# Attention and gated MLP in split fp32: a seventh pair of blocks by seven products, and edge rows kept in DRAM until the last batch

## The chip, the cores and the metric

One Trainium2 chip, one core. The metric is device time in microseconds of one execution. A lower time is better. Several runs were taken of the kernel before, and one more execution of it was profiled.

## The reference

Attention over 32 packed rows, then a gated MLP over all 4608 tokens, in fp32:

```python
p_packed = sm_attn(p, k, v)            # batch 8, heads 8, seq 576, dim 64, 32 packed rows
out = sm_attn(q, p_packed, p_packed)
x = out.transpose(0, 2, 1, 3).reshape(4608, 512)
h = x @ w_in                           # 512 x 2048
g = h * clip(h + 3, 0, 6) / 6
result = g @ w_out                     # 2048 x 512
```

## The kernel before

Each fp32 operand of a product is split into a high part and a rest (`split`: ScalarE casts the high part, L946, GpSimd subtracts it, L947), and one product becomes three matmuls: high by high, high by rest, rest by high. For each batch b the input side of the MLP is folded into the attention: `u_m` multiplies quarters of `w_in` (L350 matmuls on a tile named `w_again`) with the packed rows, so that `first_product` (L929) yields h from the attention weights of the batch. The hidden dimension of 2048 is 16 blocks f of 128.

A batch has 576 tokens. They are taken in two chunks c of 256 tokens; the 64 left over ride along in one chunk, which is then "wide" (320 columns in the first product): c = 0 in odd batches, c = 1 in even ones. The 64 last rows of an even batch and the 64 first of the next odd one make one tile of 128 "edge" rows, whose second product is done apart. After the gate (`gate_into`: ScalarE's relu L940, VectorE's product L941) `keep_edge` (GpSimd, L965) copies the 64 columns into `bnd`, 16 blocks by 128 columns of SBUF. For a pair of batches the tile `bnd` fills over a wide chunk of each of the two.

A chunk (`moe_pairs`, batch 1's second chunk to batch 7) runs over 16 steps, one block f each: first product, gate, split, and, one or two steps later (`pend`, `second`), the second product. Two consecutive blocks form a pair, whose second product goes by seven products instead of eight (`pair_product`, 21 matmuls of 256 columns, L969, into four PSUM banks A to D). That needs sums of the gated tiles (VectorE L1241, L1249, L1254) and sums of blocks of `w_out` (T1 to T4, made once by `combine`). `PAIRS` = 6 pairs run first, 0 to 5, or 5 to 0 where `down(b, c)` holds, which lets the last pair of one chunk be the first of the next; then the four blocks 12 to 15 come as singles (`single_product`, 6 matmuls of 512 columns each). Batch 1's second chunk has four pairs. First products alternate between two PSUM buffers, so the first product of a step can start only when the gate of two steps before has read its bank.

The combinations are made during batch 1, in steps that the table `TURN` gives (its numbers are steps of batch 1, 16 to a chunk; each entry advances the generator by one yield). A combination has 11 VectorE instructions, 4 casts on ScalarE (L1076) and 2 sums on GpSimd (L1072). T blocks of pairs 0, 1, 4 and 5 share two places in SBUF and are swapped through DRAM (`t_kept`, fetched by `fetch_t`, L1105, at the chunk positions in `FETCHES`).

SP issues all DMAs from one queue in the order written. Eight DMA semaphores go round: a DMA also waits for the one eight before it. The quarters of `w_in` for the next batch are fetched one at a time into one place (`w_again`, L1428), each when TensorE is done with the one before.

The edge products: batches 0 and 1 in batch 1's first chunk; batches 2 and 3 in the singles of batch 3's wide chunk ("joined", a bank J of its own, two blocks at a time through `edge_parts` and `edge_product`); batches 4 and 5 are written to DRAM (`e_kept`, one transfer of 1 MB in batch 5) and read back in batch 7, where `moe_edges`, after the first chunk of batch 7, multiplies them together with those of 6 and 7, as two tiles by the same scheme of pairs and singles.

Attention for the next batch is woven in by `fill`, called at each step, which also advances `turned` (the combinations), the fetches and `u_m` of the batch.

## Time and profile before

| | us |
|---|---|
| median of 3 runs | 711.25 |
| lowest, highest | 711.24, 712.88 |
| the profiled execution | 710.69 |
| its span | 708.8 |

| engine | busy us | share |
|---|---|---|
| TensorE, matmul (PE) | 684.8 | 97% |
| TensorE, weight load (PEld, beside PE) | 591.5 | 83% |
| VectorE (DVE) | 522.9 | 74% |
| ScalarE (ACT) | 428.3 | 60% |
| GpSimd (POOL) | 406.8 | 57% |

Times in the profile are microseconds from the span's start unless marked ns. A row of the timeline gives start, length, engine, line and operation; in brackets the idle time ahead of it and who ended it. A row of the chain gives start, length, engine and line of a piece of the chain that ended last. A group row ends in busy time and mean ns of one, then the idle time ahead. Batch 2 begins at about 210, its second chunk at 256, the second chunk of batch 4 at 423.

### The profile page before, as it was taken

Reading aid. Unit: us, or ns where it says so; the run is one execution under the profiler, and the core shown is the slowest. Engines: PE = TensorE matmul, PEld = TensorE weight load, DVE = VectorE, ACT = ScalarE, POOL = GpSimd, SP = SyncE. Lnnn points to the kernel's source line nnn. Section 1 sums busy time; section 2 is a strip of 40 time slices with the busy share of each in tenths; the row PEclk is TensorE's granted clock in tenths of the full one; section 3 lists DMA queues with packets and bytes.
Section 4 is the critical chain, followed back from the end, with each engine's and each line's share of the span. In section 5 each row is a group of like instructions: output and inputs, shape, how many; then the busy total and the mean of one; then the engine's idle time right before and its main releaser. Section 6 shows DMA issues by size and latency. Waiting matters only on the chain.

```text
span 708.8 us, 16225 instructions
## 1 busy us (share of the span) xinstructions
PE 684.8 (97%) x5924; PEld 591.5 (83%) x5924; DVE 522.9 (74%) x1125; ACT 428.3 (60%) x1004; POOL 406.8 (57%) x617
## 2 busy tenths in 40 slices
PE   6599999999999999999999999999999999999997
PEld 4377877777877888899798998898888988899996
DVE  2897788688998759775588867877597768766653
ACT  5788876455655655565366655656475655565553
POOL 2565542545644566576375746776464656676763
PEclk9799999999999999999999999999999999999999
DMA  9999853955247656464554648375655644340330
GB/s 276 288 242 244 225 124 126 260 142 130 100 143 173 161 136 209 123 170 74 133 183 144 165 88 252 120 149 137 194 203 147 167 125 150 134 164 1 120 119 30
DMA packets 199678, 111.15 MB, mean 157 GB/s; under 512 B 173488, under 2 KB 185264, under 8 KB 195760
## 3 DMA queue, kind: packets, MB, share of 16 engines
q1 hardware_dynamic: 199056, 109.94, 55.8%
q8 instruction: 46, 0.75, 0.4%
q14 instruction: 32, 0.26, 0.1%
q10 hardware_dynamic: 544, 0.20, 0.1%
HBM read 92.27 MB, written 17.83 MB: 155 GB/s over the span
## 4 chain that ended last, share of the span: by engine, by line
PE 84%; DVE 7%; DMA 5%; ACT 1%; POOL 1%; issue 1%; SPq 1%; DVEq 0%; ACTq 0%
PE acc L969 49%; PE ps_hh L929 23%; PE ps L350 6%; PE ps_h L607 3%; DMA w_again<-w_kept 2%; DMA room<-in_q_dram 1%; PE ps L470 1%; DMA wt<-t_kept 1%; PE ps L440 1%; DVE wt L1077 1%; DVE tr L555 1%; DMA p_nat<-in_p_dram 1%; DMA nat<-in_k_dram 1%; PE ps L273 1%; SPq L294 0%
## 5 line engine op out<-in xcount | busy, mean ns | idle before, releaser
L929 PE MATMUL ps_hh<-a_lo,m_hi 128*128 128x320 f32 (+1 forms) x448 | 133.6, 298 | 0.0
L929 PE MATMUL ps_hh<-a_hi,m_hi 128*128 128x320 f32 (+1 forms) x448 | 133.5, 298 | 0.0
L929 PE MATMUL ps_hh<-a_hi,m_lo 128*128 128x320 f32 (+1 forms) x448 | 132.6, 296 | 0.0
L941 DVE SCALAR_TENSOR_TENSOR t<-t,ps_hh 128x320 f32<-128x320 f32 (+1 forms) x148 | 65.8, 445 | 57.8 <-ACT t L940 57.1
L969 PE MATMUL acc<-wo_hi,g 128*128 128x512 f32 x304 | 108.3, 400 | 0.0
L940 ACT ACTIVATE t<-ps_hh,three 128x320 f32<-128x320 f32 (+1 forms) x148 | 73.4, 499 | 43.8 <-PE ps_hh L929 32.4
L947 POOL TENSOR_TENSOR ge<-t,ge 128x256 fp32r<-128x256 f32 x76 | 60.5, 796 | 63.6 <-ACT ge L946 22.6
L929 PEld LDWEIGHTS ps_hh<-a_lo,m_hi 128*128 128x128 f32 x448 | 84.8, 189 | 8.7 <-issue 5.7
L929 PEld LDWEIGHTS ps_hh<-a_hi,m_hi 128*128 128x128 f32 x448 | 84.7, 189 | 6.4 <-DVE t L941 1.3
L929 PEld LDWEIGHTS ps_hh<-a_hi,m_lo 128*128 128x128 f32 x448 | 84.7, 189 | 0.2
L969 PE MATMUL acc<-wt,ga 128*128 128x256 f32 x492 | 80.4, 284 | 0.4 <-POOL ga L947 0.4
L947 POOL TENSOR_TENSOR g<-t,g 128x256 fp32r<-128x256 f32 x72 | 55.9, 779 | 43.3 <-ACT g L946 24.7
L969 PE MATMUL acc<-wo_hi,ge 128*128 128x256 f32 x328 | 78.3, 287 | 0.8 <-ACT ge L946 0.6
L947 POOL TENSOR_TENSOR gf<-tb,gf 128x256 fp32r<-128x256 f32 x76 | 63.4, 834 | 17.1 <-ACT gf L946 6.0
L969 PEld LDWEIGHTS acc<-wt,ga 128*128 128x128 f32 x492 | 68.0, 190 | 1.2 <-POOL ga L947 0.6
L969 PEld LDWEIGHTS acc<-wo_hi,g 128*128 128x128 f32 x304 | 56.1, 189 | 11.9 <-POOL g L947 1.7
L947 POOL TENSOR_TENSOR ga<-t,ga 128x256 fp32r<-128x256 f32 x76 | 60.8, 800 | 9.0 <-ACT ga L946 8.1
L969 PEld LDWEIGHTS acc<-wo_hi,ge 128*128 128x128 f32 x328 | 57.6, 190 | 9.7 <-ACT ga L946 3.8
L965 POOL COPY bnd<-t 128x64 f32<-128x64 f32 x76 | 23.3, 307 | 67.3 <-DVE t L941 62.7
L969 PE MATMUL acc<-wo_lo,g 128*128 128x512 f32 x152 | 60.2, 396 | 0.0
L555 DVE STREAM_TRANSPOSE tr<-nat 128x576 f32<-128x576 f32 x56 | 42.4, 764 | 17.7 <-DMA nat<-in_q_dram 11.3
L940 ACT ACTIVATE tb<-ps_hh,three 128x256 f32<-128x256 f32 (+1 forms) x76 | 37.9, 498 | 24.0 <-PE ps_hh L929 21.7
(234 smaller groups left out, 1819.1 us busy)
## 6 DMA issues: line engine op xcount, KB each, us to landing
w_again<-w_kept SPq DMA_DIRECT2D x24, 1024.0 KB, 5.0
wt<-t_kept SPq DMA_DIRECT2D x26, 768.0 KB, 5.4
out_dram<-osb SPq DMA_DIRECT2D x35, 256.0 KB, 2.7
nat<-in_k_dram SPq DMA_DIRECT2D x112, 72.0 KB, 3.3
nat<-in_q_dram SPq DMA_DIRECT2D x112, 72.0 KB, 2.6
raw_out<-in_moe_w_out_dram SPq DMA_DIRECT2D x10, 512.0 KB, 5.5
raw_in<-in_moe_w_in_dram SPq DMA_DIRECT2D x10, 512.0 KB, 5.3
w_kept<-w_in_sb SPq DMA_DIRECT2D x4, 1024.0 KB, 7.6
```

What stands on the lines that cost most here:

```text
L273: nc.tensor.matmul(banks[x][NPK * a:NPK * a + NPK, :n * P], state["pp"][half, NPAIR * x + a], cols[half, :, a], start=True, stop=True,)
L350: nc.tensor.matmul(pair[x][NPK * a:NPK * a + NPK, :n], rows[half, a], c, start=True, stop=True)
L440: nc.tensor.transpose(out=pair[x][:, c * P:(c + 1) * P], in_=e[x][:, c * P:(c + 1) * P], identity=ident)
L470: nc.tensor.matmul(pair[x][cols, :D], l, r, start=(c == 0), stop=(c == NST - 1))
L555: nc.vector.transpose(out=t, in_=state.pop(("nat", which, b, a)))
L607: nc.tensor.matmul(h[:, hf, :HS], mm[:, g, fs], aa[:, hf * HS:(hf + 1) * HS], start=(g == 0 and i == 0), stop=(g == NG - 1 and i == 2),)
L929: state["first"] = nc.tensor.matmul(h[:, :n], mm[:, g, fs], aa[:, t0:t0 + n], start=(g == 0 and i == 0), stop=(g == NG - 1 and i == 2),)
L940: state["relu"] = nc.scalar.activation(out=t[:, :n], in_=h, func=AF.Relu, bias=three)
L941: state["gate"] = nc.vector.scalar_tensor_tensor(out=t[:, :n], in0=t[:, :n], scalar=6.0, in1=h, op0=ALU.min, op1=ALU.mult)
L947: nc.gpsimd.tensor_sub(out=lo, in0=x, in1=hi.bitcast(F32))
L965: nc.gpsimd.tensor_copy(out=bnd[:, f, side * REM:side * REM + REM], in_=t[:, boff:boff + REM])
L969: nc.tensor.matmul(out, lhs[x], rhs[y], start=first and i == 0, stop=last and i == 2, skip_group_check=True)
```

## The change

- `PAIRS` is 7, so that a chunk of batches 2 to 7 has seven pairs and two singles; `moe_edges` too. The order of the pairs is `ORDER` = 0, 1, 2, 6, 3, 4, 5, or its reverse.
- Pair 6 gets its own T blocks, `wt6`, in the place that `bnd`'s first 12 blocks held in batch 1 (`bnd` is now two tiles, for 12 and 4 blocks). The scratch of its combination is the place of the other four, which then becomes `stage`, a ring for eight blocks of 64 edge columns. Its row in `TURN` is (24, 25, 32, 33, 34, 35, 36): steps 24 and 25 of batch 1 and steps 0 to 4 of batch 2.
- From batch 2 to 6 `keep_edge` copies into the ring, and after each odd block SP writes two blocks, 64 KB, to `e_kept` in DRAM. Batch 7 copies into four tiles `e_last`.
- The joined edge product of batch 3 is gone. In batch 7 SP reads the edges of batches 2 and 3 (`e_old`, 1 MB at step 6), of 4 and 5 (four `e_again`) and the halves of batch 6 (into `e_last`), at steps 1 to 4. After its first chunk `last_edges` multiplies those of 6 and 7 the plain way into one bank, two blocks at a time, and then `moe_edges` those of 2, 3, 4 and 5 as two tiles.

```diff
-PAIRS = 6
+PAIRS = 7
+ORDER = (0, 1, 2, 6, 3, 4, 5)
...
-    (27, 27, 28, 28, 28, 29, 29), (29, 29, 30, 30, 30, 31, 31),
+    (27, 27, 28, 28, 28, 29, 29), (29, 29, 30, 30, 30, 31, 31), (24, 25, 32, 33, 34, 35, 36),
...
+    MOST = 12
+    ep = ctx.enter_context(tc.tile_pool(name="ep", bufs=1))
+    bnd = [ep.tile([P, n, 2 * REM], F32, name=f"bnd{i}", tag=f"bnd{i}") for i, n in enumerate((MOST, NF - MOST))]
...
-    def keep_edge(t, f, boff, side):
-        nc.gpsimd.tensor_copy(out=bnd[:, f, side * REM:side * REM + REM], in_=t[:, boff:boff + REM])
+    def keep_edge(b, t, f, boff, side):
+        cols = slice(side * REM, side * REM + REM)
+        if b == 1:
+            place = bnd_at(f, 1)[:, 0, cols]
+        elif b == FOUR + 3:
+            place = parked["last"][f // 4][:, f % 4, cols]
+        else:
+            place = parked["stage"][:, f % 8]
+        nc.gpsimd.tensor_copy(out=place, in_=t[:, boff:boff + REM])
+        if 1 < b < FOUR + 3 and f % 2:
+            two = slice(f - 1, f + 1)
+            nc.sync.dma_start(out=e_kept[b // 2, :, two, cols], in_=parked["stage"][:, f % 8 - 1:f % 8 + 1])
...
+        if i == 6:
+            t6 = ep.tile([P, 3, 2, H2], F32R, name="wt6", tag="bnd0")
+            parked["stage"] = ep.tile([P, 8, REM], F32, name="stage8", tag="bnd1")
+            for k, name in enumerate(("T1", "T2", "T4")):
+                blocks[i, name] = [t6[:, k, x] for x in range(2)]
+            x, y = (parked["stage"].rearrange("p f n -> p (f n)")[:, k * H2:(k + 1) * H2] for k in range(2))
...
+    def last_edges(j, rows):
...
+        for f in range(0, NF, 2):
+            summed = f < 2 * PAIRS
+            parts = edge_parts(edge_rows(j, f, 2), summed)
+            pend.append(lambda f=f, summed=summed, parts=parts: step(f, summed, parts))
+            second(1)
...
-        pairs = list(range(FIRST_PAIRS if b == 1 else PAIRS))
+        pairs = list(range(FIRST_PAIRS) if b == 1 else ORDER)
...
-            if joined:
-                j = f - 2 * n_pairs
-                n_single = NF - 2 * n_pairs
-                todo = [(2 * i, True) for i in range(n_pairs) if i * (n_single - 1) // n_pairs == j]
...
+                    if b == 2:
+                        for _ in range(TURN[6].count(s + 2 * NF)):
+                            next(turned[6], None)
...
-                    if b == FOUR + 1 and s == NF + 2:
-                        nc.sync.dma_start(out=e_kept, in_=bnd.rearrange("p f n -> p (f n)"))
...
+                    if b == FOUR + 3 and s in (1, 2, 3, 4):
+                        n = s - 1
+                        fs = slice(4 * n, 4 * n + 4)
+                        t = ap.tile([P, 4, 2 * REM], F32, name="e_again", tag="tr", bufs=4)
+                        parked.setdefault("mid", []).append(t)
+                        nc.sync.dma_start(out=t, in_=e_kept[FOUR // 2, :, fs])
+                        nc.sync.dma_start(out=parked["last"][n][:, :, :REM], in_=e_kept[B // 2 - 1, :, fs, :REM])
...
-                moe_edges(kept.pop("eb"), [out[x * S - REM:x * S + REM] for x in (FOUR + 1, FOUR + 3)])
+                last_edges("last", out[b * S - REM:b * S + REM])
+                moe_edges(("old", "mid"), [out[x * S - REM:x * S + REM] for x in (FOUR - 1, FOUR + 1)])
```

VectorE at the start of batch 2, from the gate of step 3 to the gate of step 5. Lines of the changed kernel are shifted: its L948, L1275, L1283, L1288 are the L941, L1241, L1249, L1254 of before. Before:

```order
L941 SCALAR_TENSOR_TENSOR tb<-tb,ps_hh 128x256
L1249 TENSOR_TENSOR t<-t,tb 128x2x128
L539 TENSOR_TENSOR m_lo<-ps_2884,m_hi 128x512
L1254 TENSOR_TENSOR tb<-tb,t 128x128
L941 SCALAR_TENSOR_TENSOR t<-t,ps_hh 128x256
L1241 TENSOR_TENSOR t<-t 128x128
L941 SCALAR_TENSOR_TENSOR tb<-tb,ps_hh 128x256
```

The same place in the changed kernel, where `stage_2598` and `wt_2597` are the scratch and the T blocks of pair 6:

```order
L948 SCALAR_TENSOR_TENSOR tb<-tb,ps_hh 128x256
L1102 TENSOR_TENSOR wt_2597<-stage_2598,wt_2597 128x256
L948 SCALAR_TENSOR_TENSOR t<-t,ps_hh 128x256
L1283 TENSOR_TENSOR t<-t,tb 128x2x128
L1120 TENSOR_TENSOR stage_2598<-wo_hi,stage_2598 128x256
L546 TENSOR_TENSOR m_lo<-ps_2897,m_hi 128x512
L1275 TENSOR_TENSOR t<-t 128x128
L1288 TENSOR_TENSOR tb<-tb,t 128x128
L1102 TENSOR_TENSOR wo_lo<-stage_2598,wo_hi 128x256
L1121 TENSOR_TENSOR stage_2598<-stage_2598,wo_lo 128x256
L948 SCALAR_TENSOR_TENSOR tb<-tb,ps_hh 128x256
```

Four instructions of the combination stand between these two gates; six more stand ahead of them (three of those ahead of the gate of step 0), one behind.

SP's queue in batch 2, from the fetches of T blocks to the last quarter of `w_in` for batch 3. In brackets stands what each waits for: DMA semaphores, and the engine. Before:

```order
L1105 DMA wt_1789<-t_kept 128x1536 [waits DMAHW1_49,PE_49]
L1105 DMA wt_1790<-t_kept 128x1536 [waits DMAHW2_49,PE_49]
L1428 DMA w_again<-w_kept 128x2048 [waits DMAHW3_49,PE_49]
L1428 DMA w_again<-w_kept 128x2048 [waits DMAHW4_49,DMAHW3_49,PE_49]
L1428 DMA w_again<-w_kept 128x2048 [waits DMAHW5_49,DMAHW4_49,PE_49]
L294 DMA nat<-in_k_dram 32x18x32 [waits DMAHW6_49,DVE_49]
```

The same stretch of the changed kernel:

```order
L1130 DMA wt_1793<-t_kept 128x1536 [waits DMAHW4_49,PE_49]
L1130 DMA wt_1794<-t_kept 128x1536 [waits DMAHW5_49,PE_49]
L983 DMA e_kept<-stage_2598 128x2x64 [waits DMAHW6_49,Pool_49]
L1447 DMA w_again<-w_kept 128x2048 [waits DMAHW7_49,PE_49]
L983 DMA e_kept<-stage_2598 128x2x64 [waits DMAHW0_49,Pool_49]
L983 DMA e_kept<-stage_2598 128x2x64 [waits DMAHW1_49,Pool_49]
L1447 DMA w_again<-w_kept 128x2048 [waits DMAHW7_49,DMAHW2_49,PE_49]
L983 DMA e_kept<-stage_2598 128x2x64 [waits DMAHW3_49,Pool_49]
L983 DMA e_kept<-stage_2598 128x2x64 [waits DMAHW4_49,Pool_49]
L1447 DMA w_again<-w_kept 128x2048 [waits DMAHW5_49,DMAHW2_49,PE_49]
L301 DMA nat<-in_k_dram 32x18x32 [waits DMAHW6_49,DVE_49]
```

Between the fetches of quarters stand edge writes that wait for GpSimd's copies, two of them ahead of the last fetch.

More of the change, by code (lines that the diff above doesn't have):

```diff
@@ L986, in acc_of, with edge_parts @@
         return ps_o.tile([P, DM], F32, name="acc", tag=f"acc{i}", bufs=1)
[L988 removed]
+    def edge_parts(raw, summed):
         j = xp.tile([P, 6 * P], F32R, name="edge", tag="raw")
         hi, lo = j[:, :3 * P], j[:, 3 * P:]
[L992 removed]
         flat = raw.rearrange("p f n -> p (f n)")
@@ L1047, in packed_attention_moe @@
     FOUR = B - 4
-    blocks, slots = {}, {}
+    blocks, slots, parked = {}, {}, {}
+    kept = {}
     def block(i, name):
@@ L1062, in combine @@
             for k, name in enumerate(("T1", "T2", "T4")):
-                for pair in range(PAIRS):
+                for pair in range(6):
                     n, at = ((0, k), (1, k), (2, k), ((2, 0, 1)[k], 3))[pair % 4]
@@ L1156, in single_product, with edge_rows, step, moe_edges @@
                     nc.sync.dma_start(out=rows[k], in_=r)
-        return bank, made, pair_product, single_product
-    def moe_edges(eb, rows):
-        pairs = list(range(PAIRS))
-        _, _, pair_product, single_product = sums_of(pairs, rows)
+        return pair_product, single_product
+    def edge_rows(j, f, n):
+        ts = parked[j]
+        each = NF // len(ts)
+        return ts[f // each][:, f % each:f % each + n]
+    def last_edges(j, rows):
+        acc = []
+        def step(f, summed, parts):
+            if not acc:
+                acc.append(acc_of(roles[3]))
+            edge_product(acc[0], f, *parts, summed, f == 0, f == NF - 2)
+            if f == NF - 2:
+                osb = gp.tile([P, DM], F32, name="osb_j", tag="g", bufs=4)
+                nc.scalar.activation(out=osb, in_=acc[0], func=AF.Copy, scale=1.0 / 6.0)
+                nc.sync.dma_start(out=rows, in_=osb)
+        for f in range(0, NF, 2):
[3 more added lines that the diff above has]
+            second(1)
+    def moe_edges(js, rows):
+        pairs = list(ORDER)
+        pair_product, single_product = sums_of(pairs, rows)
         for i in pairs:
-            ea, ob = eb[:, 2 * i:2 * i + 2], bnd[:, 2 * i:2 * i + 2]
+            ea, ob = (edge_rows(j, 2 * i, 2) for j in js)
             t, lhs = gp.tile([P, WT], F32, name="t"), {}
@@ L1209, in moe_pairs @@
         boff = 2 * P if even else 0
-        joined = wide and not even and b < FOUR
         row = b * S + t0 + off
-        bank, made, pair_product, single_product = sums_of(
+        pair_product, single_product = sums_of(
             pairs, [out[row + k * P:row + (k + 1) * P] for k in range(2)]
         )
-        edges = []
-        def edge_step(f, summed, parts):
-            if "J" not in made:
-                made["J"] = acc_of(roles[3])
-                first = True
-            else:
-                first = False
-            edge_product(made["J"], f, *parts, summed, first, f == NF - 2)
-            if f == NF - 2:
-                osb = gp.tile([P, DM], F32, name="osb_j", tag="g", bufs=4)
-                nc.scalar.activation(out=osb, in_=made["J"], func=AF.Copy, scale=1.0 / 6.0)
-                nc.sync.dma_start(out=out[b * S - REM:b * S + REM], in_=osb)
         for pos, f in enumerate(steps):
@@ L1268, in moe_pairs @@
             if wide:
-                keep_edge(t, f, boff, 1 - even)
-            if joined:
-                while edges:
-                    edges.pop(0)()
+                keep_edge(b, t, f, boff, 1 - even)
             pend.append(lambda f=f, gh=gh, gl=gl: single_product(f, gh, gl))
             second(2)
-            if joined:
-                j = f - 2 * n_pairs
-                n_single = NF - 2 * n_pairs
-                todo = [(2 * i, True) for i in range(n_pairs) if i * (n_single - 1) // n_pairs == j]
-                if j == n_single - 1:
-                    todo = [(g, False) for g in range(2 * n_pairs, NF, 2)]
-                for g, summed in todo:
-                    parts = edge_parts(g, summed)
-                    edges.append(lambda g=g, summed=summed, parts=parts: edge_step(g, summed, parts))
-        if joined:
-            pend[-1:-1] = edges
     def first_moe(chains):
@@ L1321, in edges @@
             yield
-            on(f"bl{f}", "P").tensor_copy(out=bnd[:, f, :REM].rearrange("p (n a) -> p a n", a=2), in_=rows)
+            on(f"bl{f}", "P").tensor_copy(out=bnd_at(f, 1)[:, 0, :REM].rearrange("p (n a) -> p a n", a=2), in_=rows)
             yield
```

38 lines of the change are left out of this document (21 added, 17 removed).

## The prediction

> **What bounds the kernel now.** I read the page first: busy time by engine, and the chain that ended last.
>
> ```profile
> span 708.8 us, 16225 instructions
> PE 684.8 (97%) x5924; PEld 591.5 (83%) x5924; DVE 522.9 (74%) x1125; ACT 428.3 (60%) x1004; POOL 406.8 (57%) x617
> PE 84%; DVE 7%; DMA 5%; ACT 1%; POOL 1%; issue 1%; SPq 1%; DVEq 0%; ACTq 0%
> ```
>
> TensorE is busy 97% of the span and carries 84% of the chain. Then I read the chain piece by piece through the second chunk of batch 4, a wide and steady one. Its columns are start, length, what.
>
> ```profile
> 436.84 1.02 PE ps L350 x16
> ...
> 445.10 1.02 PE ps L350 x16
> ...
> 449.85 2.49 PE acc L969 x21
> 452.33 0.88 PE ps_hh L929 x6
> 453.21 1.40 PE acc L969 x6
> ...
> 455.20 1.02 PE ps L350 x16
> ...
> 456.71 1.39 PE acc L969 x6
> ...
> 463.48 1.02 PE ps L350 x16
> ```
>
> Everything there is TensorE, end to end. The prices of the change stand in it: a pair by seven products is 21 matmuls in 2.49 us, a single block 6 matmuls in 1.39 to 1.40, so two singles cost 2.79.
>
> The third view, the timeline and the chain at the start of batch 2, shows the one place behind the first batch where TensorE waits over 1 us:
>
> ```profile
> 232.69 5.29 DMA wt<-t_kept
> 238.03 0.62 PE L969 MATMUL acc<-wt,gf 128*128 128x256 f32 x3 [1.12 <-DMA wt<-t_kept]
> ```
>
> The fourth is busy time by windows. Its columns are the window, its length, then busy time and count for PE, PEld, DVE, ACT, POOL.
>
> ```profile
> 200.20:209.85 9.65, 9.65 (x66) 7.49 (x64) 8.46 (x18) 5.29 (x14) 4.48 (x6) 1.00 0.41 166
> 209.85:218.00 8.15, 7.54 (x55) 5.50 (x54) 7.94 (x18) 4.58 (x12) 1.65 (x3) 1.00 0.49 155
> 218.00:225.00 7.00, 6.80 (x51) 6.05 (x50) 6.93 (x15) 4.11 (x12) 3.92 (x6) 1.00 1.00 265
> 435.30:453.10 17.80, 17.80 (x154) 15.80 (x154) 17.63 (x36) 11.48 (x28) 13.15 (x20) 1.00 0.52 195
> ```
>
> VectorE's 74% is an average that hides two full stretches: around 209.85, where batch 2 begins (14.87 of 15.15 us in the two rows from there), and the later half of that chunk in batch 4 (17.63 of 17.80). TensorE does not wait in the second of these. So TensorE binds, and VectorE stands right beside it exactly where the change puts work.
>
> **What the seventh pair saves.** Batches 2 to 7 have 12 chunks and the paired edge product is one more: 13 times a pair takes the place of two singles. 13 × (2.49 − 2.79) = −3.9 us by single rows. One of the singles in the list took 1.39 and others a little less; with the median spacing that the rows give (2.49/21 = 0.119 for 256 columns, 1.39/6 = 0.231 for 512) it is 13 × (2.49 − 12 × 0.231 = 2.77) = −3.6 us, which I take. The first products are unchanged. The edge products are only moved, from batch 3 to the end of batch 7, with the same matmuls but for one pair summed instead of plain, which is 3 × 0.231 + 6 × 0.119 = 1.41 against 1.39: nothing.
>
> **The wait on t_kept.** With pair 6 standing between pairs 2 and 3, the pairs that are swapped through DRAM are needed one pair later in batch 2, at least 2.49 us. The wait of 1.12 us (about 1.4 with the gap in issue around it) goes: −1.4 us. What is late next there is VectorE, below.
>
> **The seventh combination.** Weights of pair 6 must be combined once more, and the table puts this into the last two steps of batch 1 and steps 0 to 4 of batch 2. One row gives what six combinations cost:
>
> ```profile
> 95.00:225.00 130.00, 36.55 (x66) 9.71 (x24) 9.85 (x12) 1.00 0.53 150
> ```
>
> (the columns are VectorE, ScalarE, GpSimd, only instructions on the combinations' buffers): 36.55/66 = 0.554 us of VectorE apiece, 11 apiece, 6.1 us in all, with 4 casts of 0.405 on ScalarE and 2 differences of 0.82 on GpSimd. By the order 10 of the 11 stand ahead of the gate of step 5 of batch 2: 5.5 us. This falls on the full stretch, whose three rows leave 1.19 + 0.21 + 0.07 = 1.5 us free. What lies behind shows here, first VectorE's gate of step 5, then TensorE's first matmul of step 7, which takes the bank that this gate frees:
>
> ```profile
> 225.21 0.42 DVE L941 SCALAR_TENSOR_TENSOR tb<-tb,ps_hh 128x256 f32<-128x256 f32 x1
> 226.73 0.28 PE L929 MATMUL ps_hh<-a_hi,m_hi 128*128 128x256 f32 x1
> ```
>
> The gate ends at 225.63, 1.10 us ahead of its user. So TensorE is late by 5.5 − 1.10 = 4.4 us if none of VectorE's free time can be used, and by 5.5 − 1.5 − 1.1 = 2.9 if all can. Should the ten run at about 0.42, as the gate above and one of the sums below do with the same 256 columns, it is 4.2 − 2.6 = 1.6. The low end is 1.6, the high end 4.4; I take the middle of 2.9 and 4.4, since the mean of 66 already holds quick and slow ones: +3.7 us. TensorE has no slack later to win it back.
>
> **VectorE and GpSimd in the steady chunks.** A pair brings three sums on VectorE that two singles lack; the gates are the same.
>
> ```profile
> L1249 DVE TENSOR_TENSOR t<-t,tb 128x256 f32<-128x256 f32 x76 | 44.7, 589 | 1.7
> L1254 DVE TENSOR_TENSOR tb<-tb,t 128x128 f32<-128x128 f32 x76 | 37.3, 490 | 1.5
> L1241 DVE TENSOR_TENSOR t<-t 128x128 f32<-128x128 f32 x76 | 25.5, 336 | 2.1
> ```
>
> 0.589 + 0.490 + 0.336 = 1.42 us a chunk. In the second chunk of an even batch they come directly behind the full stretch. How much delay TensorE stands there shows in this gate, which ends at 451.45; the first product in its bank starts at 452.33, as quoted above:
>
> ```profile
> 451.00 0.45 DVE L941 SCALAR_TENSOR_TENSOR t<-t,ps_hh 128x320 f32<-128x320 f32 x1
> ```
>
> 0.88 us of slack. A delay of 1.42 leaves 1.42 − 0.88 = 0.5 us of waiting; nothing if VectorE's queue has emptied by then, 1.42 if it is already late. Three even batches (2, 4, 6) at 0.5 make +1.5 us; the odd ones I cost at nothing, covered by the same slack in chunks without so long a full stretch. From 0 to 5.4 us, the upper end being 3 × 1.42 and 2 × 0.54 for batches 3 and 5.
>
> That end has a reason. The same sum takes two very different times, shown here with what GpSimd does beside it:
>
> ```profile
> 436.61 0.42 DVE L1249 TENSOR_TENSOR t<-t,tb 128x256 f32<-128x256 f32 x1
> 444.89 0.95 DVE L1249 TENSOR_TENSOR t<-t,tb 128x256 f32<-128x256 f32 x1
> 437.15 0.74 POOL L947 TENSOR_TENSOR ge<-t,ge 128x256 fp32r<-128x256 f32 x1 [0.48 <-POOL bnd L965]
> 444.32 1.24 POOL L947 TENSOR_TENSOR gf<-tb,gf 128x256 fp32r<-128x256 f32 x1
> ```
>
> The quick one ran while GpSimd was idle (0.48 us up to 437.15); the slow one began inside a subtraction that ended at 445.56. The Trainium skill, "SBUF — State Buffer", section "Who interferes with whom", says that a VectorE instruction with two SBUF inputs contends with a GpSimd instruction that reads SBUF, and that the later one blocks; this trace agrees with 0.42 and 0.95 us. By that rule the seventh pair speaks against itself, since it brings sums and subtractions that can't overlap; the means above already hold such collisions at today's density.
>
> **The edge rows.** Batches 2 to 6 now write 64 KB pieces, 8 a batch, each from SP's queue behind GpSimd's copy. A piece of that size, and the weight quarters for which the same queue is used:
>
> ```profile
> v_high<-in_v_dram SPq DMA_DIRECT2D x56, 64.0 KB, 2.2
> w_again<-w_kept SPq DMA_DIRECT2D x24, 1024.0 KB, 5.0
> ```
>
> Each quarter overwrites the one before, so it can start only when that was used: first use of a batch ends at 437.86, the next begins at 445.10; the last fetch can start at 456.22 and is used at 463.48, 7.26 us later, of which 5.0 are the landing. The slack is 2.3 us, shortened by one pair's saving, and in even batches the order puts two edge writes ahead of this last fetch, whose issue then waits for GpSimd's copies. I put the wait between 0 and 1 us for each of batches 2, 4, 6, most likely nothing where the copy is early: +0.4 us. The copies themselves are there already. A copy may also wait for its slot in the ring of 8, free about 2.2 us after its write was issued if a write lands as that read does; that lies in the same bound.
>
> In batch 7 the plain edge product stands alone at the end. Its operands pass ScalarE and GpSimd:
>
> ```profile
> L946 ACT CAST edge<-bnd x22: 288/404/408, 122.0 to 347.4; 128x256 fp32r<-128x256 f32 x16, 128x128 fp32r<-128x128 f32 x6
> L947 POOL TENSOR_TENSOR edge<-bnd,edge x22: 455/736/926, 122.8 to 347.9; 128x256 fp32r<-128x256 f32 x16, 128x128 fp32r<-128x128 f32 x6
> ```
>
> (shortest, median, longest in ns). With two buffers a part can be cast only after the product two back, and has TensorE's 1.41 us of the product between: 0.404 + 0.736 + 0.455 = 1.60. That leaves up to 0.2 for each of 7 parts, or nothing for the first half of each, which needs only 1.14: 0 to 1.5 us, and I take +0.5. Its reads from DRAM are issued a chunk ahead and hidden behind it.
>
> **The sum.** −3.6 − 1.4 + 3.7 + 1.5 + 0.4 + 0.5 = +1.1 us. The profiled execution took 710.69 us, of which the span is 708.8; it becomes 711.8. The median of the runs is 711.25, 0.56 above the profiled one, so I say **712.4 us**. 0.3% is 2.1 us, about what a measurement of this kernel can tell from no change: 709.1 to 713.4 counts as the same.
>
> **The rivals.**
>
> *A, faster: the combination hides.* Its ten instructions run at 0.42 us and TensorE is late by 1.6 only; the steady chunks, the queue and the edges cost nothing. −3.6 − 1.4 + 1.6 = −3.4, 707.9 us; with the combination wholly hidden 706.3. For it: TensorE never waited in the full stretch at 435 to 453. Against: the mean of 66 is 0.554, and both windows from 209.85 on are full.
>
> *B, slower: VectorE becomes the bound in the steady chunks.* The pair's 1.42 us are paid in full in three even batches and at 0.54 in batches 3 and 5, 5.4 in place of 1.5: +5.0, 716.3 us. It decides as soon as the gates are more than 0.88 us later than now. For it: 17.63 of 17.80 us, and the collisions with GpSimd, which gains subtractions too. Against: the 0.88 us, and that the full stretch ends before the new pair's sums.
>
> *C, slower: SP's queue.* Edge writes that wait for GpSimd hold up the fetch of the last quarter by over the 2.3 us of slack, in the five batches 2 to 6, at some 0.9 each beyond my 0.4: 1.1 + 5 × 0.9 = +5.6, 716.9 us. For it: writes now stand between fetches, in order. Against: landing is 5.0 of 7.26 us.
>
> *D, slower: the change doesn't save.* If a matmul were paced by the load of its weights, more and smaller matmuls would cost more. The row for the loads:
>
> ```profile
> L969 PEld LDWEIGHTS acc<-wt,ga 128*128 128x128 f32 x492 | 68.0, 190 | 1.2 <-POOL ga L947 0.6
> ```
>
> 21 × 0.190 = 3.99 us for a pair in place of 2.77, 13 × 1.22 = +15.9 in place of −3.6: 731.9 us. Against it stands 2.49 us for the 21, loads included; they overlap. The Trainium skill, "TensorE: Matmul & The Clock Gate", section "Back-to-back issue gap", says that in a stream of loads and matmuls the spacing is set by both. Here the trace shows 0.119 us at 256 columns, under the load's 0.190, so the rule doesn't reach as far as rival D would need.
>
> **How the numbers follow.** My forecast has a chance of 0.41 with a range of its own of 709.5 to 714.5; A 0.27, B 0.20, C 0.10, D 0.02. A lies below 709.1, B, C and D above 713.4; a little of the forecast's own range falls over its upper edge. Faster 0.27, same 0.39, slower 0.34. The range goes from A to a little above B and C, where several upper ends meet: 707.4 to 717.4; it leaves out D, the lowest part of A and the sums in which B and C come together. Cases of both signs hold most of the chance, so its width is that of A and B and no less.
>
> **What would show it.** In the profile after: pairs of 2.49 us still, and 7 of them in each chunk; no wait for t_kept in batch 2; TensorE waiting for VectorE or its gates between 225 and 235 us, by 2.9 to 4.4 us; batches 3 to 6 shorter, each by 2 × 0.28 us, less waits for gates of under 0.5 us in even batches; no rows of w_again before L350; the edge product at the end with waits under 0.2 us a part. The forecast is wrong if TensorE's waits in batch 2 stay under 2 us (A), if its rows in the even batches wait for L941's successor by over a microsecond (B), if w_again's landings end TensorE's waits (C), or if 21 matmuls take over 2.6 us (D).

## The result, and the profile after

| | us |
|---|---|
| before, median of 5 runs | 712.88 (711.24 to 714.25) |
| changed, median of 5 runs | 722.27 (722.09 to 724.37) |
| ratio | 1.0144, 95% interval 1.012 to 1.0168 |
| profiled execution, changed | 723.41, span 721.6 |

The change makes the kernel slower by 1.4%, some 10 us by the ratio, where 712.4 was forecast and 717.4 was the upper end of the range. The page of the changed kernel, the same three lines as before:

```profile
span 721.6 us, 16755 instructions
PE 692.1 (96%) x6044; PEld 599.1 (83%) x6044; DVE 548.0 (76%) x1178; ACT 434.4 (60%) x1033; POOL 422.7 (59%) x643
PE 56%; DVE 25%; DMA 8%; issue 3%; POOL 3%; ACT 3%; SPq 1%; POOLq 0%; DVEq 0%; ACTq 0%
```

TensorE's share of the chain fell from 84 to 56% and VectorE's rose from 7 to 25%. What TensorE waits for from batch 2 on stands in the list of waits (sum, times, longest, in us):

```profile
PE ps_hh L936 <- DVE tb L948: 1.6, 2, 1.3
PE ps L357 <- DMA w_again<-w_kept: 1.2, 2, 0.9
PE acc L987 <- POOL ge L954: 1.0, 4, 0.4
PE acc L987 <- POOL edge L954: 0.9, 2, 0.5
...
PE acc L987 <- ACT osb_j L1200: 0.3, 1, 0.3
PE acc L987 <- DVE wt L1102: 0.2, 1, 0.2
```

The wait for t_kept is gone, as forecast. No single wait explains 10 us: it is many short ones. So I cut the trace into chunks, each from its first product to that of the next, and set the lengths side by side (us). By these cuts the second chunks of batches 2 and 4 of the kernel before begin at 249.9 and 416.4, not at 256 and 423 as said ahead of the prediction. The first product of a chunk can stand ahead of work that the program has before it: the joined edge product of batch 3 (330.7 to 352.1) lies behind the first product of batch 3's second chunk.

| chunk | before | changed |
|---|---|---|
| start to batch 1 | 117.64 | 119.00 |
| batch 1 | 92.21 | 92.67 |
| batch 2, first | 40.08 | 39.72 |
| batch 2, second (wide) | 41.55 | 43.32 |
| batch 3, first (wide) | 38.52 | 39.84 |
| batch 4, first | 35.95 | 36.56 |
| batch 4, second (wide) | 41.53 | 43.63 |
| batch 5, both | 77.95 | 78.94 |
| batch 6, first | 35.96 | 35.53 |
| batch 6, second (wide) | 41.53 | 42.98 |
| batch 7, first | 35.80 | 36.40 |
| batch 3, second, and batch 7 from its edges to TensorE's last matmul, between which the joined product moved | 106.02 | 108.91 |

Each chunk of batches 2 to 7 should have become 0.28 shorter. The three wide chunks of even batches lost 1.8, 2.1 and 1.4 instead, 5.3 in all; batch 3's wide chunk lost 1.3, the last row 2.9. The first row is no loss by the change: it lay between 117.3 and 119.3 in the seventeen traces of before, the changed kernel and the experiments, up and down without regard to their edits.

Three places in the trace show how. First, GpSimd's list of waits holds a new one, which is the ring of eight slots:

```profile
POOL stage L980 <- DMA e_kept<-stage: 12.0, 4, 3.5
```

and the chain through batch 3's wide chunk shows what hangs on it, from a write that SP issued behind a fetch of T blocks to a first product that started late:

```profile
316.57 0.36 SPq L1130
...
317.03 5.30 DMA e_kept<-stage
...
325.90 3.96 DMA nat<-in_q_dram
...
329.95 0.78 DVE tr L562
...
330.76 0.41 DVE tb L948
...
331.21 1.15 PE ps_hh L936 x6
```

GpSimd's own row at that place (in brackets its idle time before, and what ended it):

```profile
322.96 0.24 POOL L980 COPY stage<-t 128x64 f32<-128x64 f32 x1 [3.27 <-DMA e_kept<-stage]
```

The write landed 5.3 us after its issue, GpSimd's copy waited 3.27 for it, SP was held by the next edge writes, which wait for GpSimd, and so issued a load of q late, VectorE stood behind that load, and the gate behind VectorE. TensorE lost 1.5 us there. Second, the place of the attention in batch 4's second chunk. Before, the chunk began at 416.40; here is the transposition that ends the packed stage, and the first products of the next, both TensorE:

```profile
424.91 0.27 PE L480 MATMUL ps_x<-ident,pn 128*128 128x128 f32 x1
428.18 0.72 PE L350 MATMUL ps<-tr,pps 64*32 64x288 f32 x16
```

In the changed kernel the chunk began at 410.88:

```profile
415.61 0.33 PE L454 MATMUL ps_x<-ident,e 128*128 128x128 f32 x1
422.72 0.27 PE L487 MATMUL ps_x<-ident,pn 128*128 128x128 f32 x1
425.36 0.72 PE L357 MATMUL ps<-tr,pps 64*32 64x288 f32 x16
```

L480 stood 8.5 us into the chunk and now (L487) stands 11.8 into it; the products went from 11.8 to 14.5. The transposition L454 (L447 before) had its place in the chunk ahead (at 414.01) and now lies inside this one. The softmax on VectorE that follows, the full stretch of the prediction, starts 2.7 us later into the chunk. These are its last instructions in that chunk, before and in the changed kernel, 35.6 and 38.0 us into it:

```profile
451.97 0.74 DVE L524 TENSOR_TENSOR a_lo<-at,a_hi 128x576 fp32r<-128x576 f32 x1
448.90 0.75 DVE L531 TENSOR_TENSOR a_lo<-at,a_hi 128x576 fp32r<-128x576 f32 x1
```

So it ends against the chunk's last pair and the singles. Third, the plain edge product at the end, TensorE's waits and VectorE's sum of two blocks:

```profile
661.61 0.62 PE L987 MATMUL acc<-wo_hi,edge 128*128 128x256 f32 x2 [0.44 <-POOL edge L954]
665.11 0.62 PE L987 MATMUL acc<-wo_hi,edge 128*128 128x256 f32 x2 [0.45 <-POOL edge L954]
668.96 0.39 PE L987 MATMUL acc<-wo_hi,ga 128*128 128x256 f32 x1 [0.34 <-ACT osb_j L1200]
659.77 0.29 DVE L1013 TENSOR_TENSOR e_last<-e_last 128x128 f32<-128x128 f32 x1 [2.14 <-POOL edge L954]
```

The sum is written over one of the blocks that GpSimd is still reading, so it waits for GpSimd, and cast and subtraction of the sum come after it.

### The profile page after: what moved, and what is told of

Its sections match the earlier page's. It is cut to its first block, busy times and chain, and to the rows that moved or that the text cites. A ratio compares the mean times of both kernels' runs of the same rounds, so it can differ in the third digit from the quotient of the medians.

```text
span 721.6 us, 16755 instructions
## 1 busy us (share of the span) xinstructions
PE 692.1 (96%) x6044; PEld 599.1 (83%) x6044; DVE 548.0 (76%) x1178; ACT 434.4 (60%) x1033; POOL 422.7 (59%) x643
## 4 chain that ended last, share of the span: by engine, by line
PE 56%; DVE 25%; DMA 8%; issue 3%; POOL 3%; ACT 3%; SPq 1%; POOLq 0%; DVEq 0%; ACTq 0%
PE acc L987 32%; PE ps_hh L936 14%; PE ps_h L614 3%; PE ps L357 3%; DVE t L1283 2%; DMA w_again<-w_kept 2%; DVE z L522 2%; DVE m_lo L546 2%; DVE t L948 2%; DVE tr L562 1%; DVE tb L948 1%; DMA v_nat<-in_v_dram 1%; DVE z L511 1%; DMA nat<-in_q_dram 1%; DVE den L516 1%
## 5 line engine op out<-in xcount | busy, mean ns | idle before, releaser
L987 PE MATMUL acc<-wt,ga 128*128 128x256 f32 x570 | 96.7, 285 | 1.2 <-POOL ga L954 0.7
L948 DVE SCALAR_TENSOR_TENSOR t<-t,ps_hh 128x320 f32<-128x320 f32 (+1 forms) x136 | 60.7, 448 | 48.7 <-ACT t L947 47.6
L987 PE MATMUL acc<-wo_hi,ge 128*128 128x256 f32 x380 | 91.9, 287 | 1.9 <-POOL ge L954 1.0
L947 ACT ACTIVATE t<-ps_hh,three 128x320 f32<-128x320 f32 (+1 forms) x136 | 67.6, 500 | 35.2 <-PE ps_hh L936 25.6
L954 POOL TENSOR_TENSOR gf<-tb,gf 128x256 fp32r<-128x256 f32 x88 | 73.4, 834 | 25.9 <-issue 13.4
L987 PEld LDWEIGHTS acc<-wt,ga 128*128 128x128 f32 x570 | 79.8, 190 | 7.7 <-POOL ga L954 3.1
L954 POOL TENSOR_TENSOR ga<-t,ga 128x256 fp32r<-128x256 f32 x88 | 70.8, 805 | 10.7 <-ACT ga L953 9.3
L987 PE MATMUL acc<-wo_hi,g 128*128 128x512 f32 x200 | 71.6, 399 | 0.0
L987 PE MATMUL acc<-wt,gf 128*128 128x256 f32 x285 | 61.6, 283 | 0.2 <-DVE wt L1102 0.2
L948 DVE SCALAR_TENSOR_TENSOR tb<-tb,ps_hh 128x256 f32<-128x256 f32 (+1 forms) x88 | 39.1, 445 | 22.2 <-ACT tb L947 21.8
L1283 DVE TENSOR_TENSOR t<-t,tb 128x256 f32<-128x256 f32 x88 | 54.6, 621 | 1.7
L953 ACT CAST ga<-t 128x256 fp32r<-128x256 f32 x88 | 35.6, 405 | 31.1 <-DVE t L1283 26.9
```

The source lines that it names most:

```text
L947: state["relu"] = nc.scalar.activation(out=t[:, :n], in_=h, func=AF.Relu, bias=three)
L948: state["gate"] = nc.vector.scalar_tensor_tensor(out=t[:, :n], in0=t[:, :n], scalar=6.0, in1=h, op0=ALU.min, op1=ALU.mult)
L953: nc.scalar.copy(out=hi, in_=x)
L954: nc.gpsimd.tensor_sub(out=lo, in0=x, in1=hi.bitcast(F32))
L987: nc.tensor.matmul(out, lhs[x], rhs[y], start=first and i == 0, stop=last and i == 2, skip_group_check=True)
L1283: nc.vector.tensor_add(out=columns[:, :, P:], in0=ta[:, off + P:off + P + 2 * (W - P)].rearrange("p (a n) -> p a n", a=2)[:, :, :P], in1=b ...
```

## The experiments

Theories: 1, the ring; 2, VectorE is full and the seventh pair's own sums are paid for in the wide chunks; 3, SP's queue; 4, GpSimd's subtractions for the pair, which no run here tests by themselves; 5, which came up on the way, the seventh pair of the first chunk puts the attention's parts later in the second. Ratios are to the kernel before, measured beside each (medians 711.98 to 712.59), with 95% intervals. Differences between runs are taken from the ratios, unless the medians or a trace are named. "TensorE's waits" are what the starts of its matmuls lie apart beyond the median spacing (0.119, 0.147 and 0.231 us for 256, 320 and 512 columns). In e3, e5, e6, e9, e11 and e14 the edit changes the results, so these versions measure time alone.

**e1, the ring by position.**

```diff
-            place = parked["stage"][:, f % 8]
+            place = parked["stage"][:, pos % 8]
...
-            nc.sync.dma_start(out=e_kept[b // 2, :, two, cols], in_=parked["stage"][:, f % 8 - 1:f % 8 + 1])
+            nc.sync.dma_start(out=e_kept[b // 2, :, two, cols], in_=parked["stage"][:, pos % 8 - 1:pos % 8 + 1])
```

> The ring's slot is chosen by the position of the block in the chunk, not by its number, so that a slot is used again after 8 steps and not, as blocks 4, 5 and 12, 13 do now, after 2. All else is the changed kernel (722.3 us). Theory 1 (the ring: GpSimd's copy waits for the write of the slot, 12.0 us in 4 waits, and what queues behind it makes TensorE wait in the wide chunks): those chunks lost about 2.0, 1.7, 2.3 and 1.6 us of TensorE time, so some 5 to 7 us come back, 715 to 717 us, and no wait of GpSimd for e_kept is left. Theory 2 (VectorE is full there, with or without the ring): under 1 us comes back, 721.5 or more, though GpSimd's waits go.

720.81 us, 1.0125 (1.0108 to 1.0142). GpSimd's wait for e_kept is gone from its list. In the trace batch 3's wide chunk fell from 39.84 to 37.93, under the 38.52 of before, and the chunks of batches 2 to 7 by 3.5 us together; but batch 4's and 6's wide chunks were still at 43.00 and 43.52. By the medians it is 1.5 us, which these intervals hardly tell from nothing. Theory 1 is part of it, and less than expected.

**e2, six pairs, edges through DRAM.**

```diff
-PAIRS = 7
+PAIRS = 6
...
-ORDER = (0, 1, 2, 6, 3, 4, 5)
+ORDER = (0, 1, 2, 3, 4, 5)
```

and without the row of TURN for combination 6.

> The edge rows go through DRAM as in the changed kernel, but with six pairs as before, without the seventh combination. Blocks 4, 5 and 12, 13 then stand 8 steps apart, so the ring is not the matter here. Theory 1: only the edge product at the end of batch 7 costs (2.4 us of waits there), 713 to 716 us by the kernel before at 711 to 713. Theory 2: the same, since the sums of the seventh pair are gone. Theory 3 (SP's queue: writes among the fetches delay loads, whatever the ring): 717 or more.

713.36 us, 1.0020 (1.0005 to 1.0036). Theory 3 falls for six pairs: the edge rows' way through DRAM is not by itself what costs. All but 1 or 2 us of the loss comes with the seventh pair.

**e3, no seventh combination.**

```diff
-            rest(*turned[:6])
+            rest(*turned[:6])
+            parked["stage"] = ep.tile([P, 8, REM], F32, name="stage8", tag="bnd1")
+            for name in ("T1", "T2", "T4"):
+                blocks[6, name] = blocks[2, name]
```

> The seventh combination is left out; pair 6 multiplies with the T blocks of pair 2, so its results are not the reference's, and all else is the changed kernel. The prediction's term: 3.7 us less, 718.6. Its low end: 1.6 less, 720.7. The profile after (batch 2's first chunk took 39.7 us in place of 40.1 before, with the wait on t_kept gone and the pair's saving in it) speaks for 1 to 2 less.

720.70 us, 1.0125 (1.0101 to 1.0149): 1.6 less than the changed kernel by the medians, 1.1 in batch 2's first chunk by the trace (38.63 for 39.72). It is near the low end of the prediction's term, not its middle, though by the medians alone these intervals hardly tell it from nothing.

**e4, the edge sums by VectorE.**

```diff
-            nc.vector.tensor_add(out=raw[:, 0], in0=raw[:, 0], in1=raw[:, 1])
-            split(hi[:, 2 * P:], lo[:, 2 * P:], raw[:, 0])
+            both = gp.tile([P, WT], F32, name="t")[:, :P]
+            nc.vector.tensor_add(out=both, in0=raw[:, 0], in1=raw[:, 1])
+            nc.scalar.copy(out=hi[:, 2 * P:], in_=both)
+            nc.vector.tensor_sub(out=lo[:, 2 * P:], in0=both, in1=hi[:, 2 * P:].bitcast(F32))
```

> In the plain edge product at the end of batch 7 the sum of two blocks goes to a tile of its own and its rest is subtracted by VectorE, so that it need not wait for GpSimd's split of the two blocks. All else is the changed kernel. If the chain cast, subtract, add, cast, subtract of a part is what TensorE waits for (0.6 us for each two parts, and 0.3 at the first): 1.5 to 2 us less, 720.3 to 720.8. If the two buffers alone set the pace: under 0.5 us less.

720.72 us, 1.0115 (1.0091 to 1.0139), and in the trace 67.72 for 69.13 from batch 7's edges to TensorE's last matmul: 1.4 us, which is the two waits for GpSimd at 661.61 and 665.11; the last 0.5 for the bank stays. The chain of a part was the pace.

**e5, no sums in pair 6**, on top of e1.

```diff
-                    state["gate"] = nc.vector.tensor_sub(out=s3, in0=a2, in1=a1)
+                    if f != 12:
+                        state["gate"] = nc.vector.tensor_sub(out=s3, in0=a2, in1=a1)
```

and likewise for the two sums of block 13.

> On top of the ring by position (720.8 us): in pair 6 the three sums on VectorE are left out in the chunks, and ScalarE and GpSimd split the gated tiles themselves in their place, with the same sizes; the results are not the reference's. TensorE, ScalarE and GpSimd have the same instructions. Theory 2 (VectorE is the bound in the wide chunks of even batches, and the seventh pair's sums are what is paid): 12 chunks lose 1.42 us of VectorE each, and about 1.5 to 2 us of TensorE's waits in each of the three wide even chunks go, so 4 to 6 us less, 715 to 717. Theory 4 (GpSimd's subtractions for the pair, not VectorE's sums, make TensorE wait): under 1.5 us less.

720.24 us, 1.0114 (1.0096 to 1.0131), against 1.0125 of e1: no difference. I had aimed badly: in the order 0, 1, 2, 6, 3, 4, 5 pair 6 stands at steps 6 and 7 of the chunk, and the sums behind the full stretch are pair 5's. Nor is it a clean test: the order on TensorE changed with it. L487 stands 9.8 us into the second chunks of batches 4 and 6 (11.8 in e1), which took 41.61 and 42.20 for 43.00 and 43.52, while the second chunks of batches 3 and 5 grew by 1.3 and 1.2. The run says nothing on theory 2; e11 asks again.

**e6, six pairs in the wide even chunks**, on top of e1.

```diff
+        if c == 1 and b in (2, 4, 6):
+            pairs.remove(6)
```

> On top of the ring by position (720.8 us): the wide chunks of batches 2, 4 and 6 run pair 6 as two singles again (on weights of which the combination has replaced a part, so the results are not the reference's). Theory 2: the waits at the last pair and the first single go in these three chunks, about 1.6 to 2.1 us each with 0.28 of saving given up, so 4 to 5 us less, 716. If the loss is spread over all chunks: 1.2 us less at most, 719.6 or more.

719.68 us, 1.0103 (1.008 to 1.0125): 1.6 less than e1 by the ratios, within their intervals, as if the loss were spread. The trace is odd: batch 4's wide chunk has the same six pairs as before and takes 42.80, not 41.53. So what delays it comes from elsewhere. That was the end of theory 2 as the main cause, and the start of theory 5.

**e7, ring by position and edge sums by VectorE**, e1 and e4 together.

> The ring by position and the edge product with VectorE's subtraction together. If the two add up (1.5 and 1.6 us less than the changed kernel's 722.3 each): 719.2. Still slower than the kernel before, since the seventh pair's cost in the wide even chunks stands.

718.22 us, 1.0078 (1.0061 to 1.0095). They add up, to a little more than expected.

**e8, the softmax two steps earlier**, on top of e7.

```diff
-STAGES = (((0, 1), (6, 2), (19, 2)), ((0, 1), (10, 2), (19, 1)))
+STAGES = (((0, 1), (6, 2), (19, 2)), ((0, 1), (10, 2), (17, 1)))
```

> As e7, and the last part of the attention of the next batch, whose VectorE work makes the full stretch, starts at step 17 of a batch in place of 19. If the stretch's place directly ahead of the seventh pair's sums is what costs: 1 us less in each of the three wide even chunks, 716. If VectorE's work there is too much wherever it begins: within 1 us of e7.

718.76 us, 1.0081 (1.0056 to 1.0105), no difference from e7. In the trace the edit did move work: L487 stays at 11.8 us, but the last transposition of the softmax on VectorE begins 31.1 us into batch 4's second chunk in place of 35.2, and the wide chunks of batches 4 and 6 fell by 0.7 and 0.6 (batch 2's rose by 0.2). The first chunks of the same batches grew by 0.6 and 0.5 and the second ones of batches 3 and 5 by 0.4 each, so the whole gains nothing. This too speaks for the place of the attention as the cause, and shows that the time can turn up elsewhere.

**e9, six pairs in the first chunks of batches 2, 4 and 6**, on top of e7.

```diff
+        if c == 0 and b in (2, 4, 6):
+            pairs.remove(6)
```

> On top of e7 (718.2 us): the first chunks of batches 2, 4 and 6 run pair 6 as two singles (on weights of which the combination has replaced a part, so the results are not the reference's); the wide second chunks keep seven pairs. In TensorE's order the attention's parts for the next batch then stand in the second chunk where they stand with six pairs. Theory 5 (the seventh pair in the first chunk pushes those parts back, so VectorE's full stretch begins later and runs into the last pair and the singles): the second chunk's time above its own work falls from 2.3 to 2.8 us to about 1.5 in each of the three, and 2.5 to 3.5 us less in all, 715.5, though 0.28 of saving is given up three times. Theory 2 (the seventh pair's own sums in the wide chunk are what costs): they stay at 2.3 or more, and the time rises by the saving, 719.

715.77 us, 1.0047 (1.0033 to 1.006), 2.2 less than e7. With e6, e7 and e15 (below), the length of batch 4's second chunk in all four cases is in the windows of the four kernels (window, its length, busy time of PE, PEld, DVE, ACT, POOL). Six pairs in both chunks, e15:

```profile
406.30:447.83 41.53, 41.53 (x408) 35.73 (x407) 31.41 (x67) 23.53 (x55) 26.78 (x44) 1.00 0.55 160
```

Seven in the first only, e6:

```profile
407.49:450.29 42.80, 42.63 (x410) 36.04 (x409) 33.15 (x70) 23.36 (x56) 26.86 (x47) 1.00 0.53 156
```

Seven in the second only, e9:

```profile
407.71:449.44 41.73, 41.57 (x418) 36.14 (x417) 31.88 (x68) 24.59 (x59) 29.21 (x48) 1.00 0.53 160
```

Seven in both, e7:

```profile
408.24:451.23 42.99, 42.61 (x420) 36.46 (x419) 32.98 (x70) 23.94 (x58) 28.14 (x48) 1.00 0.53 156
```

A seventh pair in the chunk itself adds 0.2 us (41.73 for 41.53, 42.99 for 42.80): its own waits, 0.5, less the 0.28 that it saves. A seventh pair in the chunk ahead adds 1.27 and 1.26. The same four lengths for the three even batches:

| second chunk of | neither (e15) | first only (e6) | second only (e9) | both (e7) |
|---|---|---|---|---|
| batch 2 | 41.53 | 42.28 | 41.73 | 42.43 |
| batch 4 | 41.53 | 42.80 | 41.73 | 42.99 |
| batch 6 | 41.55 | 43.50 | 41.83 | 42.98 |

In batch 2 the pair ahead costs 0.7 both ways. In batch 6 TensorE also waits for a quarter of `w_in`, 1.7 us in e6 and 1.1 in e7, so that row isn't clean. And in e9 the transposition is back in its place, at 416.22 in a chunk that began at 407.71, 8.5 us into it:

```profile
416.22 0.27 PE L487 MATMUL ps_x<-ident,pn 128*128 128x128 f32 x1
419.49 0.72 PE L357 MATMUL ps<-tr,pps 64*32 64x288 f32 x16
```

This is theory 5, shown in batches 2 and 4: 0.7 us in the one and 1.3 in the other.

**e10, the packed stage one step earlier**, on top of e7, with all seven pairs.

```diff
-STAGES = (((0, 1), (6, 2), (19, 2)), ((0, 1), (10, 2), (19, 1)))
+STAGES = (((0, 1), (6, 2), (19, 2)), ((0, 1), (9, 2), (19, 1)))
```

> On top of e7: all seven pairs stay, and the middle part of the next batch's attention starts at step 9 in place of 10. By the order the parts of the second chunk then stand again where they stand with six pairs, though with more of them in the first chunk. Theory 5: about 1 us less in each wide even chunk, 715 to 716, unless the first chunks pay for it. Theory 2: no less than 717.5.

715.23 us, 1.0039 (1.0025 to 1.0053), 2.8 less than e7: the best of the versions with seven pairs everywhere, and still slower than before. Batch 4's second chunk takes 42.21 there, with one part of the attention more in it than before (own work 40.5, before 40.3). TensorE's waits in the three wide even chunks fell from 2.3, 2.9 and 2.9 in e7 to 1.8 each, as in e9, and the chunks by 1.7 together. Batch 7's first chunk went from 36.37 to 35.42: a wait of 1.0 for the last quarter of `w_in` is gone there. So only some 1.7 of the 2.8 is the wide chunks'.

**e11, no sums in the last pair of the second chunks**, on top of e7: as e5, for blocks 10 and 11 and c = 1 (in batch 7, whose second chunk runs in reverse, this pair is the first).

> On top of e7: in the second chunks of batches 2 to 7 the three sums of pair 5, which runs last there at steps 12 and 13, behind the full stretch, are left out and the gated tiles split in their place, so the results are not the reference's. (e5 took out the sums of pair 6, which stand at steps 6 and 7 of the chunk, where VectorE still has idle time.) TensorE's order in the wide even chunk is that of e7. Theory 2: 1.42 us of VectorE less exactly where TensorE waits: the three chunks win 1 to 1.5 us each, 714 to 715.5. Theory 5: the lateness is there before these steps; 0.5 each, 716.5 to 717.5.

714.95 us, 1.0038 (1.0023 to 1.0053), 2.9 less than e7. Theory 2's number came out in the sum, but not where it was expected: L487 stays at 11.8, batch 4's wide chunk is at 42.55 in the trace, 0.4 less than e7's, batch 2's and 6's 0.4 less too, and the second chunks of batches 3 and 5 0.5 each. That is theory 5's 0.5 a chunk, over five chunks, 2.3 in all.

**e12, the packed stage two steps earlier**, as e10 with 8.

> As e10 with the start at step 8. The order moves one part from the second chunk into the first. Theory 5: at least as good as e10 in the wide even chunks (1 to 1.5 us less each than e7), 714.5 to 716, if VectorE in the first chunks has room. Theory 2: 717.5 or more.

722.47 us, 1.0143 (1.0117 to 1.0169): 7 more than e10, against both theories. In the trace, which is of the slowest run (725.23), the first chunks pay: 40.34 and 40.46 in batches 3 and 5 for 37.93 and 38.14 in e10, 37.8 in 4 and 6 for 36.3 and 35.6. The wide chunk of batch 4 is the shortest of all at 40.84. In batches 3 and 5 some 2.0 of the lengthening is attention that moved in from the second chunks (length less TensorE's waits rose from 37.0 to 39.0). What is left are waits that grew: 2.2 in batch 1, 1.8 in batch 2's first chunk, 1.1 in each second chunk of batches 3 and 5, 0.9 in the first chunks of 5 and 6, 1.1 in batch 7's first, some 9 in all. By TensorE's list they end with ScalarE's casts, VectorE's gates and landings of `w_again` (2.1 us in three waits); I did not try which of them is behind the rest.

**e13, the old ring**, on top of e10.

> e10 (715.2 us) with the ring's slot by the number of the block again, as in the changed kernel. TensorE's order in the wide even chunk is the same. If the ring costs what the trace of e1 says: 3 to 4 us more, 718 to 719. If it costs what the medians of e1 say: 1 to 2 more, 716.5 to 717. If it was only noise: 715.

717.26 us, 1.0067 (1.0047 to 1.0087), 2.0 more than e10. GpSimd's wait is back, and batch 3's wide chunk is at 41.5 in place of 37.9:

```profile
POOL stage L980 <- DMA e_kept<-stage: 11.2, 4, 3.1
```

Not all of these 3.6 us need be the wait. The window of that chunk shows a granted clock (the third column from the end) of 0.96 in e13

```profile
292.98:334.47 41.49, 39.52 (x310) 36.49 (x309) 29.17 (x66) 24.63 (x60) 24.62 (x48) 0.96 0.67 161
```

and 1.00 in e10, and 39.52 us of TensorE at work in place of 37.92:

```profile
293.84:331.76 37.92, 37.92 (x310) 35.03 (x309) 27.83 (x65) 24.04 (x59) 24.21 (x46) 1.00 0.73 174
```

In the changed kernel the same chunk is at 1.00 throughout, with 39.84 us. So the time of the whole, 2.0, is a better measure of the ring than these two traces.

**e14, no seventh combination**, on top of e10.

> e10 with the seventh combination left out (pair 6 uses pair 2's T blocks, so the results are not the reference's). If its price adds to the rest as in e3: 1.6 us less, 713.6. If in e10 something else waits there: under 0.7 less.

714.00 us, 1.0025 (1.001 to 1.004): 1.0 less, 1.6 in batch 2's first chunk by the trace (38.11 for 39.68); batch 7's first chunk takes 0.75 more than in e10, where TensorE waits for the last quarter of `w_in` again.

**e15, six pairs and the edge sums by VectorE**, e2 with e4.

> e2 (713.4 us, 0.2% above the kernel before) with the edge product's sums on VectorE. The waits of 0.6 and 0.5 us there are all that the trace of e2 shows above the kernel before in batches 2 to 7, besides 0.5 in batch 5: 0.5 to 1 us less, 712.5, not to be told from the kernel before. If moving the edges is worth something by itself: under 711.

712.58 us, 1.0000 (0.9986 to 1.0014). Moving the edges costs nothing once their own product is mended, and brings nothing. No version that I ran beats the kernel before.

## Why the prediction was wrong

Point by point, by its terms:

- **The seventh pair's saving**, −3.6: right. By the spacings TensorE's own work fell by 13 × (12 × 0.231 − 21 × 0.119) = 3.55, with 21 matmuls for a pair as before; the median spacing of the 256 columns is 0.120 in the changed kernel, which makes it 3.3. Rival D is out.
- **The wait on t_kept**, −1.4: right, it is gone.
- **The seventh combination**, +3.7: too large. Its runs put it at 1.0 (e14) and 1.6 (e3), by batch 2's first chunk in the traces 1.6 and 1.1. The mechanism is right: the gate of step 5 stands at 229.66 and TensorE's first product of step 7 at 230.16, 18.0 and 18.5 us into the chunk, where it was 15.4 and 16.9. But nine of the ten instructions ahead took a quick time of 0.38 to 0.42, not the mean of 0.554. These rows of the changed kernel show two of the quick ones, the slow one and the gate:

```profile
222.80 0.41 DVE L1115 TENSOR_TENSOR stage<-wo_hi,stage 128x256 f32<-128x256 f32 x1
226.93 0.95 DVE L1120 TENSOR_TENSOR stage<-wo_hi,stage 128x256 f32<-128x256 f32 x1
229.32 0.41 DVE L1121 TENSOR_TENSOR stage<-stage,wo_lo 128x256 f32<-128x256 f32 x1
229.66 0.41 DVE L948 SCALAR_TENSOR_TENSOR tb<-tb,ps_hh 128x256 f32<-128x256 f32 x1
```

  It came out at the end that I had marked as low, 1.6.
- **VectorE in the steady chunks**, +1.5: the step that failed. Its size for the pair's own sums, 0.5 a wide even chunk, is what the four cases of e9 show: in e9 the three chunks stand 0.7 above the kernel before, and with the 0.84 that should have been saved this is the 1.5 of the term. In e7 they stand 3.8 above it, so 3.1 more came from elsewhere. What the term left out is that the order of a chunk is not fixed by its own steps. The term took the full stretch to stand where it stood before, with 0.88 us of slack behind it. The seventh pair of the chunk ahead moves the attention's transpositions L454 and L487 into later steps, the stretch starts 2.7 us later, and the slack is gone: 0.7, 1.26 and 1.15 us in the three chunks (e7 against e9, batch 6 not clean). By e10 against e7 moving the attention back is worth 2.8 us of the whole time, of which the traces put 1.7 in these chunks and 1.0 in batch 7's first. The odd chunks, costed at nothing, pay as well: 0.8 of waits in the second chunks of batches 3 and 5 each (e14 against e15). The order of the instructions shows this before any run: I compared it on VectorE at the start of batch 2 and in SP's queue, where I expected trouble, and not on TensorE in the wide chunk.
- **The edge rows and SP's queue**, +0.4: wrong in place and size. The fetch of the last quarter is a small part: two waits, 1.2 us in all, where the kernel before had one of 0.3. The longer one, 0.9 in batch 7's first chunk, is no hold-up by edge writes: the fetch was issued at 611.56, 0.2 us after the quarter ahead of it was used, and landed 6.7 us later, where the kernel before had 4.7 at this place. The reads of `e_last` are issued around it; that they slow it was not tried. The wait returns, at 0.8 to 1.6 us, in every run with a seventh pair but e6, e9, e10 and e13. The larger part was the ring: ORDER sets blocks 12, 13 next to 4, 5, which share slots, and the reuse after two steps made GpSimd wait 12.0 us, and SP behind it. I put this wait into the same bound of 0 to 1 us. It costs 2.0 us by e13 against e10 and 1.5 by e1; by the chunks of the trace of e1 3.5.
- **The edge product**, +0.5 with 1.5 at most: 2.7 by the trace, of which e4 gives back 1.4. (From batch 7's edges to TensorE's last matmul 55.6 us became 69.1. The product that moved there took 11.4 in batch 3, 50.44 before and 39.06 in e2, and two pairs should have saved 0.56.) The working added cast, subtraction and second subtraction, and left out that VectorE's sum and its cast stand between them, in a row.
- **Rivals.** B named the right engine and the right chunks, by the wrong step; C the right queue, by the wrong wait. Neither alone reaches 722. The cases in which B and C come together had been left out of the range, and that is the case that happened. In the chain of batch 3's wide chunk their gates lie on one path, since what holds GpSimd and SP delays the loads that VectorE waits for; in the even chunks this was not followed.

What the runs account for, in us of the whole time: the ring 2.0 (e13), the edge product 1.4 (e4 by its trace), the packed stage one step earlier 2.8 (e10; 1.0 of it the last quarter in batch 7), the combination 1.0 (e14), −3.6 saved and −1.4 for t_kept. By the ratios the loss of 10.3 falls to 5.6 with ring and edges mended (e7), 2.8 in e10 and 1.8 in e14. Since e14 has 3.6 less of TensorE's own work than the kernel before, and not its 1.4 for t_kept either, some 6 us or more are in short waits that only the traces show: 0.5 in each wide even chunk, 0.4 to 0.5 in the second chunks of batches 3 and 5 (0.8 against e15, which like e14 has no joined product there), 0.9 in batch 4's first, 0.8 in batch 7's first (the last quarter), 1.4 in the edge product that is left, and 0.3 in each of some first chunks. For the last pair's sums e11 shows 0.4 to 0.5 in five of these chunks; what ends the others I did not take apart, and the cause of this part stays open. Where e12's 7 us come from stays open as well.

## What to carry to other kernels

- A pair or block added to one chunk moves whatever is woven between its steps, and the next chunk inherits it. Compare the order of the bound engine in the chunk behind, not only in the one edited, before pricing the slack there by the old trace.
- When the order of blocks changes, every ring indexed by block number changes its distance of reuse. Index it by position.
- When two risks share a path (here GpSimd's ring and VectorE's stretch, through the loads on SP), their sum belongs in the range as one case.

## What the runs showed of the hardware

- The Trainium skill's rule cited in the prediction ("SBUF — State Buffer", "Who interferes with whom") goes on holding in the two rows shown: L1120 began inside a subtraction of GpSimd (226.80 to 227.60) and took 0.95 us, and its like L1115 began while GpSimd was idle and took 0.41. A third row is less plain: L1116 began at 224.70, 0.05 us after GpSimd's subtraction by the profile, and took 0.38, while that subtraction took 1.02. I did not run a kernel for it.
- Chunks far apart with the same order often repeat to some hundredths of a us: 41.55, 41.53, 41.53 in the kernel before and 41.53, 41.53, 41.55 in e15, while the first 118 us varied by 2.0 between traces. They don't always: e1 and e7 differ in the edge product of batch 7 alone, and batch 6's second chunk took 43.52 in the one and 42.98 in the other. So a difference of tenths that several chunks show can be told where a span or a median of few runs doesn't tell 1.5, but one chunk of one trace can be off by 0.5.
